# Two products in place of one fp32 product for three column sums, and a new place for evictions and conversions

## The chip, the core and the metric

One core of a Trainium2 chip runs the whole program. The metric is the device time in microseconds (us), the median of several executions. Engines: TensorE (PE, with its weight loads as PEld), ScalarE (ACT), VectorE (DVE), GpSimd (POOL), and SyncE (SP), which issues the transfers. ACT and DVE each work through their instructions in the order in which they stand.

## What is computed

Three stages follow each other: a chunked attention, a soft mixture of experts, and a feed-forward with a squared relu. Only the third is touched:

```
h = x @ w_in            # x: 3072 x 512, w_in: 512 x 2048
r = np.maximum(h, 0.0)
g = s * (r * r) + b
out = g @ w_out         # w_out: 2048 x 512
```

The kernel never forms x for this stage. x is c @ slot_out, with c the softmax over 32 slots of each token, so h = c @ (slot_out @ w_in). The small product slot_out @ w_in is called m. And since b is one number, g @ w_out = s * (r*r) @ w_out + b * (column sums of w_out).

## The kernel before

Tokens are cut into 8 blocks of 384, the 2048 hidden columns into 16 groups of 128. An item is one block with one group. The 128 items run in this order: blocks 0 and 1 in turn over groups 0 to 7, blocks 2 and 3 in turn over all 16, then blocks 4 to 7 one after the other, at last blocks 0 and 1 over groups 8 to 15. The loop over n near the end of the kernel is the order of everything: its step n emits, on each engine's own queue,

- PE: `emit_h(n)` (L825), one fp32r product h(n) of 384 columns into a bank of the PSUM tag `s`, which has two banks; then `emit_o(n-3)` (L877), six products of 512 columns (three token tiles with the high half `ghi` of the squares, three with the low half `glo`) against `w_hi`; then `emit_o2(n-4)` (L889), three more against `w_lo`. In the steps where a run over groups ends (n = 18 and 19, then 50, 51 and so on), or one step behind it (n = 20), `emit_o2` stands ahead of `emit_o`.
- ACT: relu (L831), the square (L835), the cast to `ghi` (L839).
- DVE: `glo` of item n-1, the square less its high half (L842).

So h(n) is written three steps ahead of its nine products. An h takes a bank of `s` that an earlier relu, or another reader, has released.

Beside this, w_out and the rest of w_in arrive as 64-bit numbers and are converted in the loop, one key every two steps until n = 47 (`cq`): `stage_a` is an ACT instruction (L579), `stage_d` parts 0 to 5 are DVE instructions (L589, L591, L593, L600 and, for w_out alone, L791 and L793), and `stage_w` is the ACT cast to `w_hi` (L798), which reads what L591 wrote. Keys n = 16 to 30 belong to w_in, n = 32 to 46 to w_out groups 8 to 15. `load_w` at the end of a step issues the next weight transfer once a step has read the last of an old one.

When a run over groups ends, the three accumulators of its block are evicted, two by DVE and one by ACT (L896, L894), and the next run's `emit_o` needs their banks.

The column sums that the title speaks of:

- m for 512 more hidden columns is made three times, at n = 4, 26 and 34 (`M_AT`). `emit_m` multiplies slot_out with w_in in four 32-row strips at once (L806, with a bf16 correction) into a bank of `s`; ACT copies it to `mps` (L808). One step later `emit_m2` adds the four strips by a product with a 128x128 pattern of ones, `stks_all`, in full fp32 (L812), into `s`; `m_split` then casts it to `mpack` on ACT (L817) and subtracts on DVE (L818). A product in full fp32 stands as two instructions in the trace, a product in fp32r as one.
- The column sums of w_out: DVE adds the 32 halves up in n = 48 to 63 (`wsum_add`, L848), and at n = 64 `colsum` multiplies by a 128x128 tile of ones in full fp32 (L852); DVE scales it to `bias` (L853).

In a step, before: h, o and o2 on PE, then `emit_m` or `emit_m2`, and only then that step's relu, square and so on. So ACT has the copy of `mps`, and the cast to `mpack`, ahead of the relu of its own step.

Of the kernel before, what the change touches and what calls it, by code (L numbers as in the profile page):

```python
# [8 lines left out]
F32 = mybir.dt.float32  # L9
F32R = mybir.dt.float32r  # L10
# [3 lines left out]
AF = mybir.ActivationFunctionType  # L14
ALU = mybir.AluOpType
# [20 lines left out]
def kernel(  # L36
# [11 lines left out]
    nc = tc.nc  # L48
# [3 lines left out]
    NT, DM = out.shape  # L52
# [9 lines left out]
    scale = 1.0 / 8.0  # L62
# [21 lines left out]
    stks_all = stk.rearrange("p a s -> p (a s)")  # L84
# [33 lines left out]
    with tc.manual_schedule():  # L118
# [45 lines left out]
        NRG, E_AT = 3, 5  # L164
        EARLY = [("wi", 2), ("wi", 3)]
        order = [("w1", i) for i in range(W1)] + [("wi", 0), ("wi", 1)] + [("w2", i) for i in range(W2)]
# [4 lines left out]
        order = order[0:-E_AT] + EARLY + order[-E_AT:]  # L171
# [9 lines left out]
        last_use = {}  # L181
# [7 lines left out]
        wnext = [0]  # L189
# [256 lines left out]
        def warm(n):  # L446
            wp = psum("lp", [128, 256])
            for _ in range(n):
                nc.tensor.matmul(out=wp, lhsT=warm_src[:, 0:128], rhs=warm_src, start=True, stop=True)
# [222 lines left out]
        def emit_sos(g, dh):  # L672
            nc.scalar.copy(out=sos_r[dh], in_=so_t[g, dh])
# [44 lines left out]
        for i in range(16):  # L718
            emit_w2(i)
            if i == 4:  # L720
                left.close()
                pk_p = ctx.enter_context(tc.tile_pool(name="pk", bufs=1, reuse_waits="tile"))
                cpack = pk_p.tile([128, NT], F32R, name="cpack")
                mpack = pk_p.tile([128, 128 * NF], F32R, name="mpack")
            if i in (3, 7, 11):
                emit_sos(i // 8, i // 4 % 2)
            if i in (4, 8, 12):
                emit_sot((i - 1) // 8, (i - 1) // 4 % 2)
            if i < 3:
                pack_prep(2 * i)  # L730
                pack_prep(2 * i + 1)
            if 5 <= i < 11:
                pack_c(i - 5)
            if i == 2:
                load_w(len(EARLY) + E_AT)
            if i == 10:
                load_w(2)
            if i == 14:
                load_w(1)
            if 11 <= i < 15:  # L740
                warm(4)
            if 7 <= i < 15:
                early(4 + (i - 7) // 2, (i - 7) % 2)

        LA = 3
        M_AT = (4, 26, 34)
# [4 lines left out]
        def tiles(name, n, w, dt=F32):  # L751
            return [g_p.tile([128, w], dt, name=f"{name}{i}") for i in range(n)]

        w_hi, w_lo = tiles("whi", NF, DM, F32R), tiles("wlo", NF, DM, F32R)
        os_g, mps = tiles("os", 3, DM), tiles("mps", 1, DM)[0]
        r_g, r2_g = (tiles(x, 2, UT) for x in ("r", "r2"))
        ghi_g, glo_g = tiles("ghi", LA + 2, UT, F32R), tiles("glo", LA + 2, UT, F32R)
        wsum, bias = tiles("wsum", 1, DM)[0], tiles("bias", 1, DM)[0]
        ones = tiles("ones", 1, 128)[0]
        nc.gpsimd.memset(ones, 1.0)  # L760
        HF = NF // 2

        runs = [[(0, 0, HF), (1, 0, HF)], [(2, 0, NF), (3, 0, NF)]]
# [18 lines left out]
        def stage_d(k, j):  # L782
            key = cq.get(k)
            if key:
                h, lf, a, w = cv[key]
                if j < 3:
                    cv_dve(key, j)
                elif j == 3:
                    cv_low(key, lf if key[0] == "o" else wi_dst([wis_l[:, 0:2], wis_l[:, 2:4]], key))
                elif key[0] == "o" and j == 4:  # L790
                    nc.vector.tensor_tensor(out=a, in0=a, in1=w_hi[key[1]].bitcast(F32), op=ALU.subtract)  # L791
                elif key[0] == "o":
                    nc.vector.tensor_tensor(out=w_lo[key[1]], in0=a, in1=lf, op=ALU.add)  # L793

        def stage_w(k):
            key = cq.get(k)
            if key and key[0] == "o":
                nc.scalar.copy(out=w_hi[key[1]], in_=cv[key][2])  # L798

        def emit_m(fb):  # L800
            wis = wis_b if fb % 2 else wis_a
            mp = psum("s", [128, 512])
            for lo in range(1 if fb == 1 else 2):
                for kc in range(KD):
                    lhsT, rhs = (soTb[:, kc, :], wis_l[:, kc, :]) if lo else (soT4[:, kc, 0, :], wis[kc // 2][:, kc % 2, :])
                    nc.tensor.matmul(out=mp[32 * kc:32 * kc + 32, :], lhsT=lhsT, rhs=rhs,  # L806
                                     start=(lo == 0), stop=(lo == 1 or fb == 1))
            nc.scalar.copy(out=mps, in_=mp)  # L808

        def emit_m2(fb):  # L810
            mr = psum("s", [128, 512])
            nc.tensor.matmul(out=mr, lhsT=stks_all, rhs=mps, start=True, stop=True)  # L812
            m_split(mr, 512 * fb, slice(0, 512))

        def m_split(mp, base, cols):
# [21 lines left out]
        def emit_ghi(n):  # L837
            if n < len(items):
                nc.scalar.copy(out=ghi_g[n % (LA + 2)], in_=r2_g[n % 2])  # L839
# [9 lines left out]

        def colsum():  # L850
            c = psum("s", [128, DM])
            nc.tensor.matmul(out=c, lhsT=ones, rhs=wsum, start=True, stop=True)  # L852
            nc.vector.tensor_scalar(out=bias, in0=c, scalar1=sbt[:, 1:2], scalar2=None, op0=ALU.mult)  # L853

        def store(b, t, os_):
# [24 lines left out]
        def emit_o2(n):  # L880
            r_, f = items[n]
            b, f0, f1 = r_
            ghi, glo = ghi_g[n % (LA + 2)], glo_g[n % (LA + 2)]
            for t in range(NTU):
                o = o_t[r_][t]
                if n == len(items) - 1:
                    for gt in (ghi, glo):
                        nc.tensor.matmul(out=o, lhsT=gt[:, 128 * t:128 * t + 128], rhs=w_hi[f], start=False, stop=False)
                nc.tensor.matmul(out=o, lhsT=ghi[:, 128 * t:128 * t + 128], rhs=w_lo[f], start=False, stop=(f == f1 - 1))  # L889
                if f == f1 - 1:  # L890
                    if b < 4 and f0 == 0:
                        to = part[b][t] if b < 2 else os_early(b - 2, t)
                        if t == 1:
                            nc.scalar.activation(out=to, in_=o, func=AF.Copy, scale=sbt[:, 0:1])  # L894
                        else:
                            nc.vector.tensor_scalar(out=to, in0=o, scalar1=sbt[:, 0:1], scalar2=None, op0=ALU.mult)  # L896
                    else:
                        os_ = os_g[t]
                        nc.vector.scalar_tensor_tensor(out=os_, in0=o, scalar=sbt[:, 0:1], in1=part[b][t] if f0 else bias,
                                                       op0=ALU.mult, op1=ALU.add)  # L900
                        store(b, t, os_)
# [12 lines left out]
        def stages(n, *js):  # L914
            for j in js:
                stage_d(n, j)


        cp = (nc.scalar.copy, nc.vector.tensor_copy)
        sot = psum("g", [128, 2, 4, 32])  # L920
# [3 lines left out]
        for k in range(2):  # L924
# [3 lines left out]
                  in_=sot[:, k:k + 1, :, 0:4].to_broadcast([128, 4, 4, 4]))  # L928
# [39 lines left out]
        for n in range(LA + 1, len(items) + LA + 1):  # L968
            if n > 7:
                emit_h(n)  # L970
            m = n - LA - 1
            ends = 0 <= m and items[m][1] == items[m][0][2] - 1
            late = m + 1 < len(items) and m + 1 == 2 * HF + 1
            if ends or late:
                emit_o2(m)
            if 1 < m + 1 < len(items):
                emit_o(m + 1)
            if m > 1 and not ends and not late:
                emit_o2(m)
            if LA + 1 < n <= 7:  # L980
                emit_h(n)
            if n == 6:
                nc.vector.tensor_copy(out=soTb, in_=soT4[:, :, 0, :])
            if n in M_AT:
                emit_m(M_AT.index(n) + 1)
            if n - 1 in M_AT:
                emit_m2(M_AT.index(n - 1) + 1)
            emit_relu(n)
            emit_sq(n)
            stage_a(n + 1)  # L990
            emit_ghi(n)
            if LA + 1 < n <= len(items):
                emit_g(n - 1)
            stage_d(n, 1)
            stage_w(n)
            stages(n, 2, 3)
            stages(n - 1, 4, 5)
            stage_d(n + 1, 0)
            if 48 <= n < 64:
                for i in (2 * n - 96, 2 * n - 95):  # L1000
                    wsum_add(i)
            if n == 64:
                colsum()
            if 65 <= n < 77:
                add_bias(n - 65)
            while wnext[0] < len(order) and last_use.get(order[wnext[0] - NRG], -1) <= n:
                load_w(1)


# [70 lines left out]
```

## Time and profile before

| | us |
|---|---|
| median of 3 executions | 480.83 |
| lowest and highest | 479.24, 481.24 |
| the profiled execution: its time | 479.52 |
| its span, first to last instruction | 477.7 |
| busy in the span: PE, ACT, DVE, POOL | 456.7, 308.7, 310.1, 84.4 |

The times are those of whole executions; the span is what the trace covers, here 1.8 us less than that execution's own time. Busy time on PE counts matmuls whose ends the profile models. A row of the timeline gives the start in us, the duration in us, the engine, the line, the tiles as out<-in, and in brackets how long the engine had stood idle and who ended it. `x2` or `x4` says that rows in a row were merged.

### The profile page before, as it was taken

What the parts mean: (1) busy time and instruction counts of PE and PEld (TensorE: products, weight loads), DVE (VectorE), ACT (ScalarE), POOL (GpSimd) and SP (SyncE); (2) the same over time, 40 slices, a digit from 0 to 9 for tenths busy, and PEclk for the clock granted to TensorE, in tenths of its full rate; (3) what the DMA queues carried; (4) which work ended last, traced back from release to release, by engine and by line L of the source; (5) the groups of instructions that cost most, each with busy time, mean ns of one, the idle gap of its engine ahead of it and who ended that gap; (6) DMA issues with size and microseconds to landing.
All of it is one profiled execution on the core that took longest, in us unless ns stands there. A gap on an engine that the chain in (4) does not pass through costs nothing.

```text
span 477.7 us, 10206 instructions
## 1 busy us (share of the span) xinstructions
PE 456.7 (96%) x3960; PEld 342.3 (72%) x3960; DVE 310.1 (65%) x685; ACT 308.7 (65%) x635; POOL 84.4 (18%) x154
## 2 busy tenths in 40 slices
PE   7899998999999999999898999999999999999996
PEld 5666666665555467868585888888888888888885
DVE  6778887885485889997484999975524224223232
ACT  4566666675144388888576897666666666666660
POOL 6666665650000000000000000007700000000000
PEclk9999999999999999999999999999999999999999
DMA  8999999999999934234222000003101001001011
GB/s 304 385 406 405 406 409 398 397 381 396 401 420 392 414 128 151 89 99 166 88 89 88 1 1 0 1 0 146 55 0 67 0 1 67 0 1 66 1 67 66
DMA packets 20576, 83.04 MB, mean 174 GB/s; under 512 B 2736, under 2 KB 2864, under 8 KB 14640
## 3 DMA queue, kind: packets, MB, share of 16 engines
q1 hardware_dynamic: 20528, 82.39, 44.6%
q8 instruction: 31, 0.51, 0.4%
q14 instruction: 17, 0.14, 0.1%
HBM read 76.09 MB, written 6.29 MB: 172 GB/s over the span
## 4 chain that ended last, share of the span: by engine, by line
PE 69%; DVE 13%; DMA 8%; ACT 4%; issue 3%; SPq 2%; POOL 1%; DVEq 0%; POOLq 0%; ACTq 0%
PE g L877 11%; PE lp L877 5%; PE pt L877 5%; PE x L877 5%; PE g L889 5%; PE xt L877 5%; PE s L825 4%; DMA seg<-in_w_dram 4%; PE s L630 3%; PE x L325 3%; DMA vals<-in_vm_dram 3%; PE lp L889 3%; PE pt L889 3%; PE xt L889 3%; PE x L889 3%
## 5 line engine op out<-in xcount | busy, mean ns | idle before, releaser
L842 DVE TENSOR_TENSOR glo<-r,ghi 128x384 fp32r<-128x384 f32 x128 | 76.3, 601 | 81.6 <-ACT ghi L839 81.4
L831 ACT ACTIVATE r<-s 128x384 f32<-128x384 f32 x128 | 62.8, 491 | 52.8 <-PE s L825 52.4
L835 ACT ACTIVATE r<-r 128x384 f32<-128x384 f32 x128 | 67.4, 527 | 6.2 <-DVE glo L842 2.0
L839 ACT CAST ghi<-r 128x384 fp32r<-128x384 f32 x128 | 65.7, 513 | 3.4
L825 PE MATMUL s<-cpack,mpack 128*128 128x384 f32 x128 | 44.2, 348 | 3.7 <-ACT r L831 2.1
L301 ACT ACTIVATE seg<-seg 128x384 f32<-128x384 f32 x32 | 28.8, 900 | 19.2 <-DVE seg L312 15.1
L889 PE MATMUL g<-wlo,ghi 128*128 128x512 f32 x128 | 40.2, 394 | 0.0
L877 PE MATMUL g<-whi,ghi 128*128 128x512 f32 x126 | 39.7, 394 | 0.2 <-DVE mpack L818 0.2
L877 PE MATMUL g<-whi,glo 128*128 128x512 f32 x126 | 39.3, 393 | 0.0
L864 POOL TENSOR_TENSOR keys<-keys,bias 128x512 f32<-128x512 f32 x6 | 8.4, 1426 | 168.7 <-DVE bias L853 168.7
L263 POOL TENSOR_SCALAR keys<-keys 64x416 f32<-64x416 f32 x63 | 33.7, 536 | 12.7 <-DMA keys<-in_kq_dram 7.5
L285 PE MATMUL s<-keys 128*32 128x128 f32 x768 | 30.3, 291 | 4.4 <-POOL keys L267 3.4
L825 PEld LDWEIGHTS s<-cpack,mpack 128*128 128x128 f32 x128 | 23.9, 188 | 13.0 <-ACT r L831 4.4
L325 PE MATMUL x<-vals,seg 128*32 128x128 f32 x744 | 28.0, 275 | 2.8 <-DMA vals<-in_vm_dram 2.0
L325 PEld LDWEIGHTS x<-vals,seg 128*32 128x32 f32 x744 | 20.3, 109 | 13.2 <-DVE seg L309 6.4
L889 PEld LDWEIGHTS g<-wlo,ghi 128*128 128x128 f32 x128 | 24.0, 188 | 5.3
L877 PEld LDWEIGHTS g<-whi,glo 128*128 128x128 f32 x126 | 23.7, 188 | 5.3
L285 PEld LDWEIGHTS s<-keys 128*32 128x32 f32 x768 | 19.5, 113 | 10.4 <-POOL keys L267 6.0
L319 ACT COPY seg<-pt 128x384 f32<-128x384 f32 x32 | 15.3, 478 | 17.9 <-PE pt L317 16.9
L877 PEld LDWEIGHTS g<-whi,ghi 128*128 128x128 f32 x126 | 23.7, 188 | 4.3 <-DVE mpack L818 0.7
L877 PE MATMUL lp<-whi,ghi 128*128 128x512 f32 x63 | 25.5, 404 | 0.9 <-DVE vals L896 0.9
L877 PE MATMUL pt<-whi,ghi 128*128 128x512 f32 x64 | 25.6, 400 | 0.0
(255 smaller groups left out, 991.1 us busy)
## 6 DMA issues: line engine op xcount, KB each, us to landing
seg<-in_w_dram SPq DMA_DIRECT2D x27, 1024.0 KB, 8.5
keys<-in_kq_dram SPq DMA_DIRECT2D x32, 396.0 KB, 7.4
vals<-in_vm_dram SPq DMA_DIRECT2D x64, 192.0 KB, 6.5
keys<-in_w_in_dram SPq DMA_DIRECT2D x5, 1024.0 KB, 5.1
keys<-in_w_out_dram SPq DMA_DIRECT2D x5, 1024.0 KB, 4.9
out_dram<-os SPq DMA_DIRECT2D x18, 256.0 KB, 2.1
vals<-in_w_in_dram SPq DMA_DIRECT2D x3, 1024.0 KB, 5.6
vals<-in_w_out_dram SPq DMA_DIRECT2D x3, 1024.0 KB, 4.9
```

Source lines behind the costliest of these rows:

```text
L263: (nc.vector if h and u == 0 else nc.gpsimd).tensor_scalar(out=stream(kz[rows, h], 0, CH), in0=k[rows, UT * h:UT * h + (NCU + 1) * CH].rea ...
L285: nc.tensor.matmul(out=o, lhsT=qt[:, 32 * c:32 * c + 32], rhs=kz[:, :, at:at + WIN], start=True, stop=not (first or last))
L301: nc.scalar.activation(out=p_r[u], in_=sm_r[u].rearrange("p t h (a r) -> p t r (h a)", a=2), func=AF.Exp, scale=scale)
L319: nc.scalar.copy(out=pts_r[u], in_=pt)
L325: nc.tensor.matmul(out=xp[32 * r:32 * r + 32, t], lhsT=pts_r[u][:, 32 * c:32 * c + 32], rhs=vbuf[u // 2 % 2][:, u % 2, :, 64 * c:64 * c + ...
L825: nc.tensor.matmul(out=hq, lhsT=mpack[:, 128 * f:128 * f + 128], rhs=cpack[:, b * UT:(b + 1) * UT], start=True, stop=True)
L831: nc.scalar.activation(out=r_g[n % 2], in_=h_t.pop(n), func=AF.Relu)
L835: nc.scalar.activation(out=r2_g[n % 2], in_=r_g[n % 2], func=AF.Square)
L839: nc.scalar.copy(out=ghi_g[n % (LA + 2)], in_=r2_g[n % 2])
L842: nc.vector.tensor_tensor(out=glo_g[n % (LA + 2)], in0=r2_g[n % 2], in1=ghi_g[n % (LA + 2)].bitcast(F32), op=ALU.subtract)
L877: nc.tensor.matmul(out=o_t[r_][t], lhsT=gt[:, 128 * t:128 * t + 128], rhs=w_hi[f], start=(f == r_[1] and gt is ghi), stop=False)
L889: nc.tensor.matmul(out=o, lhsT=ghi[:, 128 * t:128 * t + 128], rhs=w_lo[f], start=False, stop=(f == f1 - 1))
```

## The change

Four edits.

1. The strip sums at n = 26 and 34 and the column sums of w_out at n = 64 become two fp32r products (`sum_of`). `halves` makes the operand: ACT casts to fp32r (`mph`), DVE subtracts that from the source (`mpl`). The stationary patterns are held as fp32r too, `stkr` and `onesr`; ACT writes them earlier, in step i = 4 of the loop over w2 in the second stage. The sum at n = 4 keeps its fp32 product and only copies into `os_g[0]` instead of `mps`.
2. For n > 7, `emit_m` and `emit_m2` (now `sums`) are emitted behind that step's relu, square, `stage_a` and `ghi`, and ahead of `glo` and of the conversion.
3. The conversion of n = 18 (`convert`) and the weight load behind it move to step 19, behind the `emit_o2` that ends the second run and its evictions.
4. `bias` takes the memory of `wsum`; POOL no longer writes a tile of ones.

```diff
+                stkr = pk_p.tile([128, 128], F32R, name="stkr")
+                onesr = pk_p.tile([128, 128], F32R, name="onesr")
+                nc.scalar.copy(out=stkr, in_=stks_all)
+                nc.scalar.activation(out=onesr, in_=stks_all, func=AF.Copy, scale=0.0, bias=1.0)
...
-        os_g, mps = tiles("os", 3, DM), tiles("mps", 1, DM)[0]
+        os_g, (mph, mpl) = tiles("os", 3, DM), tiles("mp", 2, DM, F32R)
...
-        wsum, bias = tiles("wsum", 1, DM)[0], tiles("bias", 1, DM)[0]
-        ones = tiles("ones", 1, 128)[0]
-        nc.gpsimd.memset(ones, 1.0)
+        wsum = tiles("wsum", 1, DM)[0]
+        bias = wsum
...
-            nc.scalar.copy(out=mps, in_=mp)
+            if fb == 1:
+                nc.scalar.copy(out=os_g[0], in_=mp)
+            else:
+                halves(mp)
+
+        def halves(x):
+            nc.scalar.copy(out=mph, in_=x)
+            nc.vector.tensor_tensor(out=mpl, in0=x, in1=mph.bitcast(F32), op=ALU.subtract)
+
+        def sum_of(out, lhsT):
+            for x in (mph, mpl):
+                nc.tensor.matmul(out=out, lhsT=lhsT, rhs=x, start=(x is mph), stop=(x is mpl))
...
-            nc.tensor.matmul(out=mr, lhsT=stks_all, rhs=mps, start=True, stop=True)
+            if fb == 1:
+                nc.tensor.matmul(out=mr, lhsT=stks_all, rhs=os_g[0], start=True, stop=True)
+            else:
+                sum_of(mr, stkr)
...
-            nc.tensor.matmul(out=c, lhsT=ones, rhs=wsum, start=True, stop=True)
+            halves(wsum)
+            sum_of(c, onesr)
...
+        def convert(n):
+            stage_d(n, 1)
+            stage_w(n)
+            stages(n, 2, 3)
+            stages(n - 1, 4, 5)
+            stage_d(n + 1, 0)
...
+            if n == 2 * HF + 3:
+                convert(n - 1)
             if 1 < m + 1 < len(items):
                 emit_o(m + 1)
...
-            if n in M_AT:
-                emit_m(M_AT.index(n) + 1)
-            if n - 1 in M_AT:
-                emit_m2(M_AT.index(n - 1) + 1)
+            if n <= 7:
+                sums(n)
             emit_relu(n)
             emit_sq(n)
             stage_a(n + 1)
             emit_ghi(n)
+            if n > 7:
+                sums(n)
...
-            stage_d(n, 1)
...
+            if n != 2 * HF + 2:
+                convert(n)
...
-            while wnext[0] < len(order) and last_use.get(order[wnext[0] - NRG], -1) <= n:
+            while n != 2 * HF + 2 and wnext[0] < len(order) and last_use.get(order[wnext[0] - NRG], -1) <= n:
```

How the instructions stand on the engines, at the places the prediction speaks of. ACT at n = 34 and 35, before: the copy to `mps` is first, then the three instructions of item 34 (relu, square, ghi), the cast to `w_hi`, the cast to `mpack`, and relu of item 35.

```order
L808 COPY mps_2657<-s 128x512
L831 ACTIVATE r_2658<-s 128x384
L835 ACTIVATE r_2660<-r_2658 128x384
L839 CAST ghi_2666<-r_2660 128x384
L798 CAST whi_2631<-keys 128x512
L817 CAST mpack<-s 128x512
L831 ACTIVATE r_2659<-s 128x384
```

The same place now:

```order
L848 ACTIVATE r_2663<-s 128x384
L852 ACTIVATE r_2665<-r_2663 128x384
L856 CAST ghi_2671<-r_2665 128x384
L817 CAST mp_2661<-s 128x512
L801 CAST whi_2635<-keys 128x512
L848 ACTIVATE r_2664<-s 128x384
L852 ACTIVATE r_2666<-r_2664 128x384
L579 ACTIVATE seg_99<-keys 128x512
L856 CAST ghi_2667<-r_2666 128x384
L834 CAST mpack<-s 128x512
```

Item 34 now comes ahead of the evicting cast, and item 35 ahead of `mpack`; the cast to `w_hi` stays ahead of relu of item 35.

DVE at n = 33 and 34 now (before, the row L818 is not there and the rest stands in the same order): `glo` of item 33 and the conversion of key 34 (L591, L593, L600) come behind the subtraction that makes `mpl`.

```order
L589 TENSOR_SCALAR keys<-keys 128x512
L818 TENSOR_TENSOR mp_2662<-s,mp_2661 128x512
L859 TENSOR_TENSOR glo_2675<-r_2666,ghi_2670 128x384
L591 SCALAR_TENSOR_TENSOR keys<-vals_103,keys 128x512
L593 TENSOR_SCALAR keys<-keys 128x512
L600 SCALAR_TENSOR_TENSOR keys<-vals_103,keys 128x512
L835 TENSOR_TENSOR mpack<-s,mpack 64x512
```

So on DVE a wait for ACT's cast, and through it for `emit_m`, now stands ahead of L591, whose result ACT's cast to `w_hi` needs.

DVE at the end of the first two runs (n = 18 to 20), before: the evictions of the second run (`lp`, `g`) stand behind the conversion of key 18.

```order
L896 TENSOR_SCALAR part_2678<-xt,cstt 128x512
L842 TENSOR_TENSOR glo_2669<-r_2661,ghi_2664 128x384
L591 SCALAR_TENSOR_TENSOR seg_99<-keys 128x2x256
L593 TENSOR_SCALAR keys<-seg_99 128x512
L600 SCALAR_TENSOR_TENSOR seg_101<-keys 128x2x256
L896 TENSOR_SCALAR vals_104<-lp,cstt 128x512
L896 TENSOR_SCALAR vals_104<-g,cstt 128x512
L842 TENSOR_TENSOR glo_2670<-r_2660,ghi_2665 128x384
```

Now:

```order
L914 TENSOR_SCALAR part_2680<-xt,cstt 128x512
L859 TENSOR_TENSOR glo_2674<-r_2666,ghi_2669 128x384
L914 TENSOR_SCALAR vals_104<-lp,cstt 128x512
L914 TENSOR_SCALAR vals_104<-g,cstt 128x512
L591 SCALAR_TENSOR_TENSOR seg_99<-keys 128x2x256
L593 TENSOR_SCALAR keys<-seg_99 128x512
L600 SCALAR_TENSOR_TENSOR seg_101<-keys 128x2x256
L859 TENSOR_TENSOR glo_2675<-r_2665,ghi_2670 128x384
```

The two evictions have passed the three conversion instructions; the rows around the five are the same.

## Rows read from the trace of the kernel before

**Rows 1.** Busy us by engine (count), then PEclk, DMA share, GB/s, two stretches.

```profile
226.50:260.00 33.50, 30.00 (x140) 21.51 (x139) 19.70 (x36) 21.38 (x45) 0.00 (x0) 1.00 0.27 94
260.00:287.00 27.00, 27.00 (x121) 22.29 (x120) 26.38 (x51) 23.92 (x49) 0.00 (x0) 1.00 0.00 1
```

**Rows 2.** Timeline: start, us, engine, line, tiles [idle before]; h(26), its follower.

```profile
226.85 0.34 PE L825 MATMUL s<-cpack,mpack 128*128 128x384 f32 x1
227.02 0.40 PE L877 MATMUL lp<-whi,ghi 128*128 128x512 f32 x1
```

**Rows 3.** Timeline of steps 26 to 28: m, h(27), the strip sum, h(28).

```profile
230.08 0.40 PE L806 MATMUL s<-seg 128*32 128x512 bf16 x4
230.52 0.59 ACT L808 COPY mps<-s 128x512 f32<-128x512 f32 x1 [3.54 <-PE s L806]
231.16 0.45 PE L825 MATMUL s<-cpack,mpack 128*128 128x384 f32 x1 [0.68 <-ACT mps L808]
231.44 0.40 PE L877 MATMUL pt<-whi,ghi 128*128 128x512 f32 x1
...
233.50 1.02 PE L812 MATMUL s<-mps,stk 128*128 128x512 f32 x2
234.56 0.59 ACT L817 CAST mpack<-s 128x512 fp32r<-128x512 f32 x1 [1.96 <-PE s L812]
235.18 0.69 DVE L818 TENSOR_TENSOR mpack<-s,mpack 64x512 fp32r<-64x512 f32 x1 [3.97 <-ACT mpack L817]
235.59 0.44 PE L825 MATMUL s<-cpack,mpack 128*128 128x384 f32 x1 [1.07 <-ACT r L831]
```

**Rows 4.** Timeline of steps 34 to 39: h(34), a conversion, h(36), h(39), relus 37, 38.

```profile
249.24 0.34 PE L825 MATMUL s<-cpack,mpack 128*128 128x384 f32 x1
249.89 0.68 DVE L591 SCALAR_TENSOR_TENSOR keys<-vals,keys 128x512 int32<-128x512 int32 x1
254.90 0.62 ACT L798 CAST whi<-keys 128x512 fp32r<-128x512 f32 x1
258.01 0.44 PE L825 MATMUL s<-cpack,mpack 128*128 128x384 f32 x1 [1.07 <-ACT r L831]
262.18 0.48 ACT L831 ACTIVATE r<-s 128x384 f32<-128x384 f32 x1
264.10 0.48 ACT L831 ACTIVATE r<-s 128x384 f32<-128x384 f32 x1
264.87 0.34 PE L825 MATMUL s<-cpack,mpack 128*128 128x384 f32 x1
```

**Rows 5.** Timeline of steps 18 to 21: key 18, evictions, the next run, h(21).

```profile
211.28 0.69 DVE L591 SCALAR_TENSOR_TENSOR seg<-keys 128x512 int32<-128x512 int32 x1
212.62 0.40 PE L889 MATMUL xt<-wlo,ghi 128*128 128x512 f32 x1
213.07 0.75 DVE L896 TENSOR_SCALAR vals<-lp,cstt 128x512 f32<-128x512 f32 x1
213.73 0.74 DVE L896 TENSOR_SCALAR vals<-g,cstt 128x512 f32<-128x512 f32 x1
213.87 0.50 PE L877 MATMUL lp<-whi,ghi 128*128 128x512 f32 x1 [0.85 <-DVE vals L896]
214.38 0.55 DVE L842 TENSOR_TENSOR glo<-r,ghi 128x384 fp32r<-128x384 f32 x1
215.56 0.34 PE L825 MATMUL s<-cpack,mpack 128*128 128x384 f32 x1
```

**Rows 6.** Timeline of step 64: ghi(64), the column sums, the product behind h(65).

```profile
322.83 0.51 ACT L839 CAST ghi<-r 128x384 fp32r<-128x384 f32 x1
323.63 1.02 PE L852 MATMUL s<-wsum,ones 128*128 128x512 f32 x2
324.66 0.39 PE L877 MATMUL pt<-whi,ghi 128*128 128x512 f32 x1
```

**Rows 7.** Timeline of the second stage where the two patterns are now written.

```profile
146.85 0.33 ACT L684 COPY keys<-g 128x64 f32<-128x64 f32 x2 [0.83 <-PE g L679]
```

More of the change, by code (lines that the diff above doesn't have):

```diff
@@ L916, in stages, with sums @@
                 stage_d(n, j)
+        def sums(n):
+            if n in M_AT:
+                emit_m(M_AT.index(n) + 1)
+            if n - 1 in M_AT:
+                emit_m2(M_AT.index(n - 1) + 1)
+        def convert(n):
[4 more added lines that the diff above has]
+            stage_d(n + 1, 0)
         cp = (nc.scalar.copy, nc.vector.tensor_copy)
@@ L991 @@
             emit_ghi(n)
+            if n > 7:
+                sums(n)
             if LA + 1 < n <= len(items):
                 emit_g(n - 1)
-            stage_d(n, 1)
[L995 to L998, printed above, removed]
+            if n != 2 * HF + 2:
+                convert(n)
             if 48 <= n < 64:
```

## The prediction, made before the changed kernel ran

> **What bounds the kernel now.** I read the table of stretches first. From 260 to 287 us PE is busy all 27.00 us, and DVE 26.38; from 226.5 to 260, where two sums of m fall, PE is idle 3.50 of 33.50, at the full clock (1.00, that is 2.4 GHz) [rows 1]. So PE sets the time, and what a change takes off PE's queue, busy or idle, comes off the end, as long as ACT and DVE keep up. Then I read the timeline at the four places that the diff touches and looked at what PE waits for.
>
> The units first. From h(36) to h(39) are three steps in 6.86 us [rows 4], of which 0.11 is the late start of a stalled h: after a stall the next product follows h by 0.28 (231.16 to 231.44 [rows 3]), otherwise by 0.17 [rows 2]. So a step takes 2.25, and each of its nine 512-column products (2.25 - 0.17) / 9 = 0.23. On ACT and DVE an instruction that doesn't read its forerunner starts some 0.09 before that one's recorded end (0.75 long, next 0.66 later [rows 5]); one that waits for another engine starts 0.03 behind it, PE about 0.05 behind.
>
> **A: the end of the first two runs, n = 18 to 20.** PE finishes the products of `emit_o2(16)` at 212.62 + 0.23 = 212.85, but starts the next run at 213.87, because DVE evicts `lp` at 213.07 and `g` at 213.73, behind the three instructions of key 18 that began at 211.28 [rows 5]. Now the evictions take the place of those three: `lp` 211.28 to 212.03, `g` 211.94 to 212.68. Both are over before PE asks for them (212.85 and, two products later, 213.31). Then h(21) follows six products later, at 212.85 + 6 x 0.23 = 214.23, instead of 215.56: **1.33 gained**. DVE's five instructions are the same five, so `glo` at 214.38 stays; its user, the fourth product behind h(21), comes at 214.23 + 0.17 + 0.69 = 215.09, just behind its end at 214.93. Key 18 is finished 1.3 us later, and the weight load behind it moves on SP's queue by as much; nobody reads that buffer for several steps. Nothing below zero, then; the ends are 0 and 1.33.
>
> **B: the sum at n = 26.** The last part of `emit_m` starts at 230.08, and PE could go on about 0.25 later, say at 230.35. Before, h(27) waits for the copy of `mps` and its next product comes at 231.44 [rows 3]. Now the bank that h(27) takes is released by relu(26), which runs during step 26, while ACT had 3.54 idle. So h(27) starts at 230.35, the next product at 230.52: 0.92 won. Nine products later, at 232.60, PE comes to the strip sum. By then `mph` is cast (230.52 plus 0.59, by L817's row) and `mpl` subtracted (231.14 to 231.83, by L818's row, 0.69 for 64 partitions; L591's 0.68 on all 128 says that partitions don't matter) [rows 3, 4]: 0.7 to spare. The two products take 0.46; the fp32 one with h behind it took 324.66 - 323.63 = 1.03, so 0.86 by itself [rows 6], and 0.40 is saved. Then h(28) waited 1.07 for relu(27), which stood behind `mpack` [rows 3]; now relu(27) runs ahead of `mpack`, at about 231. So h(28) starts at 233.06 and its follower at 233.23, where it was 235.59 + 0.28 = 235.87: **2.64 gained** in all.
>
> **C: the sum at n = 34.** The same, with one difference: w_out's key 34 is converted here. T = 249.24 is h(34), against 226.85 [rows 2, 4], so m's cast starts at 249.24 + 3.67 = 252.91 and `mpl` runs from 253.53 to 254.22. Behind it on DVE are `glo`(33) from 254.13 (0.55) and L591 from 254.59 (0.68) to 255.27. Before, L591 ran at 249.89, long before `w_hi`'s cast at 254.90 [rows 4]. Now this cast waits until 255.30, takes 0.62, and relu(35) behind it runs from 255.83 to 256.31. h(36) waits for that, where PE could have had it at 255.45: h(36) at 256.36, follower 256.64, against 258.29 before: 1.65. Next, `mpack`: it stands where relu(36) stood, one relu, square, `stage_a` and `ghi` behind relu(35), 1.92 by relu(37) to relu(38) [rows 4], so at 257.75, and relu(36) ends at 258.25 + 0.48 = 258.73. h(37) takes the bank of h(36) (the banks go out in the order in which the code releases them), and wants it at 256.64 + 9 x 0.23 = 258.71: about on time. DVE's subtraction for `mpack` starts at 257.75 + 0.59 + 0.03 = 258.37, where before it started at 257.60 (0.41 ahead of h(36), as 235.18 is ahead of h(28) [rows 3]). So the DVE and ACT work behind it is 0.8 later while PE is 1.65 earlier. How much slack is there? relu(37) ended at 262.66 and h(39), which needs its bank, came at 264.87: 2.16 [rows 4]. 2.16 - 0.8 = 1.35, less than 1.65. So the gain here is capped at **1.35**. It doesn't shrink further: two steps of DVE work, seen as 26.38 in 27.00, still fit. Ends: 0.9 (the chain 0.45 later) and 2.64 (no chain, as in B); I take 1.35, which the rows of this very place give.
>
> **D: the column sums at n = 64.** Before, nothing is waited for: PE runs from `emit_o2` into the product at 323.63 [rows 6]. Now the cast of `wsum` stands behind `ghi`(64), which ends at 323.34: cast 323.25 to 323.87 (0.62, by the `w_hi` cast of the same size [rows 4]), subtraction 323.90 to 324.59, second product 324.64, h(65) at 324.98, its follower at 325.15 against 324.66: **0.49 lost**. The shorter product saves 0.40 and two waits cost 0.9. Ends: 0.3 and 0.7 lost.
>
> **E, at nothing.** ACT writes `stkr` and `onesr` in a place where it stood idle 0.83 for PE [rows 7]; each is smaller than a `ghi` cast of 0.51 [rows 6]. If that cover failed, up to 1.0 would be lost, though the stage ahead of the loop would have to be bound by ACT. POOL's missing tile of ones, the shared memory of `bias` and the other target of the first sum cost and save nothing: nobody waited for them.
>
> The sum: 1.33 + 2.64 + 1.35 - 0.49 = 4.83. Behind n = 65 PE has no other sum, and every later eviction moves along. The profiled execution's 479.52 becomes 474.7; it lay 1.31 below the median of the three, and against that median, 480.83, I predict **476.0**. Half a per cent, 2.4 us, is about what a measurement of this kernel can tell from no change.
>
> **The rivals.** *The halves come too late.* In place of `mps` PE waits for `mpl`, a chain through two engines. For it: two more links, and DVE has other work queued. Against it: 0.7 to spare in B. Each us beyond that costs one us in B and in C; with 1.0 in each, 2.8 are left: 478.0.
>
> *The evictions change nothing.* If PE's bank at 213.87 is held by something else than the two evictions (ACT's third of the second run, say), A gives 0: 3.5 left, 477.3. The brackets name DVE [rows 5].
>
> *The cast to `w_hi` holds nobody.* If C goes like B, 6.1 are gained: 474.7. The order of the rows speaks against it.
>
> *DVE and ACT are the bound.* DVE's 26.38 of 27.00 [rows 1] speaks for it: then what PE wins by n = 34 it loses again by n = 47, waiting for relu and `glo`, and about 1 us is left of it all: 480. Against it: the slack of 2.16 that h(39) still has.
>
> *Slower: the clock.* The trace shows 1.00 through every stall there is now, the longest 1.07 on PE [rows 1, 3]. The changed kernel has a new one at D, up to 0.7, and shorter ones elsewhere. Should the granted clock fall there to 1.2 GHz, nine products would take 9 x 0.23 = 2.1 us more per step, and three steps, some 13 us at the low level, would cost 6.3: 482.3. From 4.83 / 2.1 = 2.3 steps on the kernel is slower than before. The Trainium skill (TensorE: Matmul & The Clock Gate, section "Why this matters for your kernels") warns that idle gaps between bursts of matmuls drop the clock to half; the trace's stalls did not, and the new ones are no longer.
>
> **How the numbers follow.** My forecast gets 0.58, the late halves 0.15, the idle evictions 0.10, the free `w_hi` cast 0.08, DVE and ACT as the bound 0.06, the clock 0.03. The first four lie between 474.3 and 478.3 with the ends above (C at 0.9 and 2.64, D at 0.3 and 0.7) and the spread of the runs, and hold about 8 in 10; that is the range. All four are faster by more than 2.4 us but for the tail of the late halves: 0.88 faster, 0.09 within half a per cent (DVE and ACT as the bound, and that tail), 0.03 slower.
>
> **What would show it.** A: no idle time on PE ahead of the run that starts in `lp`, and h(21) 1.3 earlier behind h(20). B: h(27) and h(28) without idle time, h(26) to h(28) in 6.2 instead of 8.74. C: idle time of some 0.9 ahead of h(36), put down to a relu, and `w_hi`'s cast waiting for L591; a little ahead of h(37) to h(39). D: PE idle 0.3 and 0.4 ahead of the two products. I am wrong if PE waits for `mpl` at n = 27 or 35, or if idle time on PE between n = 37 and 47 adds up to over 1 us.

## The result, and the profile after

| | before | after |
|---|---|---|
| median, us (6 executions each) | 480.39 | 475.42 |
| lowest and highest, us | 479.24, 481.32 | 474.58, 476.47 |
| the profiled execution: its time, its span, us | 479.52, 477.7 | 475.71, 473.9 |
| h(17) starts, us | 204.72 | 205.60 |
| from there to the end of the span, us | 272.98 | 268.30 |

The ratio of the times is 0.990, with a 95% interval of 0.988 to 0.992: faster by 4.97 us, and by the interval 3.8 to 5.9. The loop from h(17) on is 4.68 shorter; the profiled execution shows only 3.81 of that because its loop began 0.88 later (experiment f0 below takes this up).

The stretches that answer [rows 1], from just ahead of h(26) to just ahead of h(37) and 27 us on; columns as there:

```profile
226.04:255.46 29.42, 28.80 (x140) 21.61 (x139) 18.33 (x35) 20.91 (x44) 0.00 (x0) 1.00 0.23 77
255.46:282.46 27.00, 27.00 (x121) 21.84 (x119) 26.36 (x49) 22.04 (x46) 0.00 (x0) 1.00 0.08 35
```

The same eleven steps take 29.42 us, where they took 33.50, and PE stands idle 0.62 of it, not 3.50; the clock stays at 1.00 in both. The next stretch has PE busy throughout and DVE at 26.36, as before.

The view of waits, for PE, from 200 to 330 us (engine, line, who ended the wait: us in total, times, longest). Before:

```profile
PE s L825 <- ACT r L831: 2.1, 2, 1.1
PE s L825 <- ACT mps L808: 1.4, 2, 0.7
PE lp L877 <- DVE vals L896: 0.9, 1, 0.9
```

After:

```profile
PE s L842 <- ACT r L848: 0.6, 1, 0.6
PE s L822 <- DVE mp L818: 0.2, 1, 0.2
```

All five waits before are gone; two short ones are new, one for relu(35) and one for `mpl` at n = 64. Now the four places. The end of the first two runs, which answers [rows 5]:

```profile
212.14 0.75 DVE L914 TENSOR_SCALAR vals<-lp,cstt 128x512 f32<-128x512 f32 x1
212.80 0.74 DVE L914 TENSOR_SCALAR vals<-g,cstt 128x512 f32<-128x512 f32 x1
213.46 0.69 DVE L591 SCALAR_TENSOR_TENSOR seg<-keys 128x512 int32<-128x512 int32 x1
213.72 0.39 PE L895 MATMUL lp<-whi,ghi 128*128 128x512 f32 x1
215.08 0.34 PE L842 MATMUL s<-cpack,mpack 128*128 128x384 f32 x1
```

The evictions end at 212.89 and 213.54, L591 comes behind them, and the run that starts in `lp` has no idle time in brackets.

The sum at n = 26 to 28, which answers [rows 3]:

```profile
229.62 0.40 PE L809 MATMUL s<-seg 128*32 128x512 bf16 x4
229.95 0.44 PE L842 MATMUL s<-cpack,mpack 128*128 128x384 f32 x1
230.06 0.59 ACT L817 CAST mp<-s 128x512 fp32r<-128x512 f32 x1 [1.70 <-PE s L809]
230.23 0.40 PE L895 MATMUL pt<-whi,ghi 128*128 128x512 f32 x1
230.68 0.69 DVE L818 TENSOR_TENSOR mp<-s,mp 128x512 fp32r<-128x512 f32 x1 [4.11 <-ACT mp L817]
232.28 0.64 PE L822 MATMUL s<-mp,stkr 128*128 128x512 f32 x2
232.75 0.34 PE L842 MATMUL s<-cpack,mpack 128*128 128x384 f32 x1
```

Neither h(27) at 229.95 nor h(28) at 232.75 waits, and `mpl` ends at 231.37, 0.91 ahead of the products.

The sum at n = 34, which answers [rows 4]: L591 of key 34, the cast to `w_hi`, relu(35), h(36), `mpack`, relu(36), `mpack`'s subtraction, then the cast of key 36, relu(37), h(39):

```profile
251.65 0.68 DVE L591 SCALAR_TENSOR_TENSOR keys<-vals,keys 128x512 int32<-128x512 int32 x1
252.37 0.62 ACT L801 CAST whi<-keys 128x512 fp32r<-128x512 f32 x1 [1.82 <-DVE keys L591]
252.90 0.48 ACT L848 ACTIVATE r<-s 128x384 f32<-128x384 f32 x1
253.43 0.44 PE L842 MATMUL s<-cpack,mpack 128*128 128x384 f32 x1 [0.62 <-ACT r L848]
254.79 0.58 ACT L834 CAST mpack<-s 128x512 fp32r<-128x512 f32 x1
255.27 0.49 ACT L848 ACTIVATE r<-s 128x384 f32<-128x384 f32 x1
255.40 0.69 DVE L835 TENSOR_TENSOR mpack<-s,mpack 64x512 fp32r<-64x512 f32 x1 [1.88 <-ACT mpack L834]
259.44 0.62 ACT L801 CAST whi<-seg 128x512 fp32r<-128x512 f32 x1 [1.60 <-DVE seg L591]
259.96 0.48 ACT L848 ACTIVATE r<-s 128x384 f32<-128x384 f32 x1
260.50 0.44 PE L842 MATMUL s<-cpack,mpack 128*128 128x384 f32 x1
```

ACT stands 1.82 for L591, and relu(35) behind its cast keeps h(36) waiting. Behind the late subtraction of `mpack`, L591 of key 36 is late too: its cast waits 1.60, and relu(37) behind it is over at 260.44, 0.06 ahead of h(39), which takes its bank. The column sums at n = 64, which answer [rows 6]:

```profile
318.93 0.61 ACT L817 CAST mp<-wsum 128x512 fp32r<-128x512 f32 x1
319.57 0.69 DVE L818 TENSOR_TENSOR mp<-wsum,mp 128x512 fp32r<-128x512 f32 x1 [2.22 <-ACT mp L817]
319.59 0.49 PE L822 MATMUL s<-mp,onesr 128*128 128x512 f32 x1
320.32 0.50 PE L822 MATMUL s<-mp,onesr 128*128 128x512 f32 x1 [0.23 <-DVE mp L818]
```

The first product comes 0.51 behind the start of the product ahead of it (319.08), where 0.23 is usual, and the second 0.73 behind the first: 0.28 and 0.50 late. The brackets show less, since they count from the modelled end of the product ahead.

### The profile page after: what moved, and what is told of

It is laid out like the page before. It is cut to its first block, busy times and chain, and to the rows that moved or that the text cites. A ratio compares the mean times of both kernels' runs of the same rounds, so it can differ in the third digit from the quotient of the medians.

```text
span 473.9 us, 10204 instructions
## 1 busy us (share of the span) xinstructions
PE 455.1 (96%) x3960; PEld 342.1 (72%) x3960; DVE 311.3 (66%) x688; ACT 308.0 (65%) x638; POOL 83.9 (18%) x153
## 4 chain that ended last, share of the span: by engine, by line
PE 73%; DMA 12%; DVE 6%; ACT 3%; SPq 2%; POOL 2%; issue 1%; DVEq 0%; POOLq 0%; ACTq 0%
PE g L895 12%; PE lp L895 6%; PE pt L895 6%; PE g L907 6%; PE x L895 6%; DMA vals<-in_vm_dram 6%; PE xt L895 6%; PE s L842 5%; DMA seg<-in_w_dram 3%; PE pt L907 3%; PE s L630 3%; PE lp L907 3%; PE xt L907 3%; PE x L907 3%; DMA keys<-in_kq_dram 3%; PE x L325 2%
## 5 line engine op out<-in xcount | busy, mean ns | idle before, releaser
L882 POOL TENSOR_TENSOR keys<-keys,wsum 128x512 f32<-128x512 f32 x6 | 8.4, 1422 | 193.8 <-DVE wsum L871 193.8
L907 PE MATMUL pt<-wlo,ghi 128*128 128x512 f32 x64 | 25.4, 396 | 0.2 <-DVE wlo L796 0.2
```

## The experiments

The difference of two medians is known to about 1 us either way here (e1's interval is 1.8 us wide, f3's 3.5), but one timeline gives a stretch of the loop to some 0.04: that is the most by which A to D differ between kernels that the edits leave alike there. So each kernel is read twice: by its time, and by five lengths out of its own timeline. A is h(20) to h(21); B is h(26) to the product that follows h(28); C is h(34) to the product that follows h(39); D is h(64) to the product that follows h(66); "loop" is h(17) to the end of the span, known to some 0.05, as the page gives the span to 0.1. All in us:

| kernel | A | B | C | D | loop | h(17) starts |
|---|---|---|---|---|---|---|
| before | 3.58 | 9.03 | 15.81 | 5.53 | 272.98 | 204.72 |
| after | 2.23 | 6.54 | 14.49 | 6.04 | 268.30 | 205.60 |
| e1, evictions alone | 2.26 | 9.02 | 15.77 | 5.52 | 271.66 | 205.64 |
| e2, order alone | 3.58 | 6.93 | 13.70 | 5.53 | 268.76 | 205.34 |
| e3, fp32r alone | 3.56 | 9.03 | 15.79 | 6.02 | 273.44 | 204.86 |
| e4, after, key 34 first | 2.24 | 6.54 | 13.29 | 6.04 | 267.10 | 207.90 |
| f0, after once more | 2.24 | 6.54 | 14.50 | 6.04 | 268.30 | 207.00 |
| f1, order and evictions | 2.23 | 6.93 | 13.70 | 5.53 | 267.41 | 205.79 |
| f2, after, late column sums | 2.24 | 6.54 | 14.50 | 5.17 | 267.41 | 205.59 |
| f3, after, both mends | 2.23 | 6.54 | 13.30 | 5.17 | 266.29 | 206.91 |

The first four ran on one chip, with a before of 480.56 (median of 23), the last four on another with 479.50 (median of 11).

**e1: the evictions alone.** On the kernel before:

```diff
+            if n == 2 * HF + 3:
+                convert(n - 1)
             if 1 < m + 1 < len(items):
                 emit_o(m + 1)
...
+            if n != 2 * HF + 2:
+                convert(n)
```

> The kernel before with the third edit alone: key 18's conversion and the weight load behind it stand behind the evictions of the second run. Theory: the 1.35 us that the changed kernel gained between h(20) and h(21) belong to this edit, so h(20) to h(21) takes 2.23 instead of 3.58 and the whole time falls by 1.35, to 479.0 from 480.4. Rival, that the gain needs the other edits or is given back behind n = 21: no change, 480.4.

Measured: 478.94, ratio 0.997 (0.995 to 0.999). A falls by 1.32 and the loop by 1.32; B, C and D are as before (to 0.04). In PE's waits the row for `lp` is gone and the two rows for h remain as they were. So edit 3 carries A by itself, and nothing of it is given back.

**e2: the order alone.** On the kernel before, with `mps` and all products in full fp32:

```diff
+            if n <= 7:
+                sums(n)
             emit_relu(n)
             emit_sq(n)
             stage_a(n + 1)
             emit_ghi(n)
+            if n > 7:
+                sums(n)
```

> The kernel before with the second edit alone: the sums of m at n = 26 and 34 stand behind relu, square and ghi; all three products stay full fp32, and no high and low part is made. Theory: the place of the sums carries the gain at both of them. At n = 26 the changed kernel won 2.48 us from h(26) to the follower of h(28); the fp32 product costs 0.40 more, so 2.1 here. At n = 34 no subtraction stands ahead of L591, so w_hi's cast doesn't wait and it goes as at n = 26: 2.1. Together 4.2, 476.2 us. Rival, that the late mpack caps the gain at n = 34 here too (1.36 less 0.40): 3.0, 477.4. Rival, that the two fp32r products carry the gain: under 1, above 479.5.

Measured: 475.94, ratio 0.991 (0.990 to 0.993). B falls by 2.10, C by 2.11, the loop by 4.22; the rivals would have shown 3.0 or under 1. From n = 22 to 64 PE's view of waits has no row left. Why C does as well as B stands in ACT's and PE's timeline at n = 34 to 36:

```profile
251.42 0.59 ACT L808 COPY mps<-s 128x512 f32<-128x512 f32 x1 [1.69 <-PE s L806]
251.90 0.62 ACT L798 CAST whi<-keys 128x512 fp32r<-128x512 f32 x1
252.42 0.49 ACT L831 ACTIVATE r<-s 128x384 f32<-128x384 f32 x1
253.65 1.02 PE L812 MATMUL s<-mps,stk 128*128 128x512 f32 x2
254.10 0.74 PE L825 MATMUL s<-cpack,mpack 128*128 128x384 f32 x1
```

The cast to `w_hi` follows the copy without a wait, relu(35) is over at 252.91, and h(36) at 254.10 follows the sum at once. The order alone wins more at C (2.11) than the whole change does (1.32).

**e3: the fp32r products alone,** in the old place; the changed kernel without edits 2 and 3:

```diff
-            if n <= 7:
-                sums(n)
+            sums(n)
             emit_relu(n)
...
-            if n > 7:
-                sums(n)
```

> The kernel before with the first and the fourth edit alone: two fp32r products with a high and a low part at n = 26, 34 and 64, in the old place ahead of relu. Theory: the products by themselves win nothing. Each strip sum is 0.40 shorter, but h(27) and h(35) now wait for the subtraction (0.69 behind the cast) or for the relu behind the cast (0.4 later) where they waited for the cast alone: 0 to 0.3 lost at each; at n = 64 0.48 is lost as in the changed kernel. Together 0.5 to 1.1 slower than before: 480.9 to 481.5 us. Rival, that the shorter products count in full: 0.8 won, 0.48 lost, 480.1.

Measured: 480.27, ratio 1.001 (0.999 to 1.002). By the time it can't be told from before; the loop is 0.46 longer, just below the 0.5 to 1.1 expected, and all of it lies in D (0.49). B and C are unchanged to 0.02. The timeline at n = 26 to 28:

```profile
230.63 0.58 ACT L817 CAST mp<-s 128x512 fp32r<-128x512 f32 x1 [3.55 <-PE s L809]
231.11 0.50 ACT L848 ACTIVATE r<-s 128x384 f32<-128x384 f32 x1
231.66 0.44 PE L842 MATMUL s<-cpack,mpack 128*128 128x384 f32 x1 [1.07 <-ACT r L848]
234.00 0.63 PE L822 MATMUL s<-mp,stkr 128*128 128x512 f32 x2
235.71 0.44 PE L842 MATMUL s<-cpack,mpack 128*128 128x384 f32 x1 [1.07 <-ACT r L848]
```

h(27) now waits 1.07 for the relu behind the cast, where it waited 0.68 for the copy [rows 3]: 0.39 lost, which the shorter sum wins back.

**e4: key 34 first.** On the changed kernel, L591 of key 34 ahead of `mpl`'s subtraction:

```diff
             if n > 7:
+                if n == M_AT[2]:
+                    stage_d(n, 1)
                 sums(n)
...
-            stage_d(n, 1)
+            if n != M_AT[2]:
+                stage_d(n, 1)
```

> The changed kernel with L591 of key 34 on DVE ahead of the subtraction that makes mpl at n = 34, not behind it and glo(33). Theory: w_hi's cast waited 1.82 us for L591, and held relu(35) and so h(36) (idle 0.62); that made the gain at n = 34 only 1.36 where n = 26 gave 2.48. Without it h(34) to the follower of h(36) goes as h(26) to that of h(28), 6.54 instead of 7.42, and 1.1 us is won over the changed kernel: 474.3. Rival, that mpack, which still stands ahead of relu(36), or DVE's load caps it at n = 34 to 39: 475.4, as the changed kernel.

Measured: 475.58, ratio 0.991 (0.989 to 0.993); the median is no better than the changed kernel's, against 474.3 expected. But C is 1.20 shorter and the loop 1.20; what hides it is h(17), which began at 207.90 in the profiled execution (and at 206.7 in the median of the six, worked out as under f0, against 205.3 in the changed kernel). ACT, DVE and PE at n = 34 to 36:

```profile
252.71 0.62 ACT L801 CAST whi<-keys 128x512 fp32r<-128x512 f32 x1
252.85 0.69 DVE L818 TENSOR_TENSOR mp<-s,mp 128x512 fp32r<-128x512 f32 x1 [3.37 <-ACT mp L817]
254.45 0.64 PE L822 MATMUL s<-mp,stkr 128*128 128x512 f32 x2
254.92 0.34 PE L842 MATMUL s<-cpack,mpack 128*128 128x384 f32 x1
```

The cast waits for nobody, `mpl` still ends 0.91 ahead of the products, and h(36) comes without a wait. `mpack` stands ahead of relu(36) here too, and DVE has the same work; neither costs anything. So the wait of one cast for one DVE instruction was all that kept C under B.

**f0: the changed kernel once more.**

> The changed kernel once more, beside the three that follow. By theory all of its gain lies in the loop, from h(17) to the end of the span: 4.7 us less than the 272.98 of before. When h(17) starts (204.72 before, 205.60 after, 204.86 to 207.90 in the four experiments so far, with and without the two patterns) is set by the last waits of the second stage for its weights, and differs from run to run; so the median comes out 4.2 to 5.2 below before. Rival, that the two new patterns delay the loop: h(17) lies later here than in the kernels without them, and the median gain falls short of the loop's.

Measured: 475.81, ratio 0.991 (0.989 to 0.994), 3.69 below this chip's before of 479.50: less than the 4.2 to 5.2 expected, which is what the rival would show. Its loop is 268.30, equal to that of the first profile to 0.01 (the traces hold the two spans as 475.308 and 473.898), though h(17) began 1.40 later. If the loop is that constant, each execution's span less the loop of its kernel tells when its h(17) began: 204.2 to 209.9, median 205.75, in 42 executions of kernels with the two patterns, and 204.1 to 208.2, median 205.44, in 57 without. A difference of 0.3 is less than one execution differs from the next. But the two chips disagree: on the first, e3 and e4 with the patterns have a median of 205.5, and before, e1 and e2 without them 205.6; on the second, f0, f2 and f3 have 206.1, and before and f1 205.0. So the times alone don't settle whether the patterns cost anything. The timelines say more. Waits of PE late in the second stage, before, after and in e4, one row from each:

```profile
161.73 1.07 PE L668 MATMUL xt<-seg,seg 128*32 128x256 f32 x16 [0.28 <-DMA seg<-in_w_dram]
```

```profile
162.57 1.07 PE L668 MATMUL xt<-seg,seg 128*32 128x256 f32 x16 [0.83 <-DMA seg<-in_w_dram]
```

```profile
159.88 1.07 PE L668 MATMUL xt<-seg,seg 128*32 128x256 f32 x16 [1.18 <-DMA seg<-in_w_dram]
```

They are waits for the weights of the second stage, which differ from run to run: in all 0.6 before, 1.2 after and 3.0 in e4. They are not the whole of it: in f0 PE is 1.05 of the 1.40 behind already at 142.90, its row of 141.85 in the first profile, ahead of these waits. One thing there differs between profiles: the granted clock of the first 20 us is 0.83 in e2, e4, f0, f1 and f3, and 1.00 in the other five. And ACT in the changed kernel, where the patterns are written, which answers [rows 7]:

```profile
146.85 0.30 ACT L727 CAST stkr<-stk 128x128 fp32r<-128x128 f32 x1 [0.54 <-PE xt L668]
147.05 0.31 ACT L728 ACTIVATE onesr<-stk 128x128 fp32r<-128x128 f32 x1
147.26 0.31 ACT L684 COPY keys<-g 128x64 f32<-128x64 f32 x2
148.73 0.58 ACT L653 CAST cpack<-lp 128x512 fp32r<-128x512 f32 x1 [1.16 <-PE lp L651]
```

The two take 0.4 together, and ACT stands idle 1.16 for PE soon after. PE was 0.29 later than before at its row of 138.98 (138.69 before), ahead of the patterns, and is 0.29 later at 161.13 (160.84 before), behind them: between the two nothing is lost. The other profiles agree: from PE's row that waits for ACT's L632 (141.55 before) to its first L449 (157.49 before), with the patterns' place between them, it takes 15.93 to 15.95 in all ten. So PE loses nothing to the two patterns in this stretch. Why h(17) lies later with them on the second chip stays open; no run has the patterns alone.

**f1: order and evictions, no halves.** The edits of e1 and e2 together on the kernel before.

> The second and third edit together on the kernel before, all products in full fp32 as before: the changed kernel without its high and low parts. Theory: the fp32r products lose more than they win. The order alone gave 2.10 at n = 26 and 2.12 at n = 34, the evictions 1.32, and n = 64 costs nothing: 5.5 over before, 0.8 more than the changed kernel: 474.9 where before has 480.4. Rival, that the parts add up to less when put together, or that the fp32r products pay: 475.6 or above.

Measured: 474.49, ratio 0.988 (0.986 to 0.991). The loop is 5.57 shorter than before and 0.89 shorter than the changed kernel's. The parts add up (1.32 + 4.22 = 5.54), and the fp32r products as the change has them cost: 0.39 won in B, 0.79 lost in C, 0.51 in D.

**f2: late column sums.** On the changed kernel:

```diff
         def colsum():
             c = psum("s", [128, DM])
-            halves(wsum)
             sum_of(c, onesr)
...
             if n == 64:
+                halves(wsum)
+            if n == 65:
                 colsum()
```

> The changed kernel with the two products of the column sums one step later, at n = 65; the cast and the subtraction stay at n = 64. Theory: the 0.48 lost at n = 64 were two waits of 0.9 for the cast and the subtraction against 0.40 saved; a step later both halves are long done, h(64) to the follower of h(66) goes without a wait, and the loop is 0.9 shorter than in the changed kernel: 474.6. Rival, that the cast ahead of relu(65), or a bank of s held until the scaling to bias, brings the wait back: 475.4, as the changed kernel.

Measured: 475.38, ratio 0.991 (0.989 to 0.994). The median, expected at 474.6, again can't be told from the changed kernel's; the loop is 0.89 shorter, all of it in D:

```profile
318.91 0.62 ACT L817 CAST mp<-wsum 128x512 fp32r<-128x512 f32 x1
319.56 0.69 DVE L818 TENSOR_TENSOR mp<-wsum,mp 128x512 fp32r<-128x512 f32 x1 [2.22 <-ACT mp L817]
321.56 0.64 PE L822 MATMUL s<-mp,onesr 128*128 128x512 f32 x2
322.03 0.34 PE L842 MATMUL s<-cpack,mpack 128*128 128x384 f32 x1
```

The halves are made at the same time as in the changed kernel and are over at 320.25, 1.3 ahead of the products, which now run without a wait. Against before D is 0.36 shorter: that is the fp32r product's own saving.

**f3: both mends,** the edits of e4 and f2 on the changed kernel.

> The changed kernel with both mends: L591 of key 34 ahead of the subtraction, and the column sums' products at n = 65. Theory: evictions 1.35, n = 26 2.48, n = 34 2.51, n = 64 0.40: 6.7 in the loop, 2.0 more than the changed kernel: 473.7 where before has 480.4. Rival, that DVE or ACT becomes the bound once PE is no longer held: the waits of PE between n = 36 and 64 then give back what the mends win, 475.4.

Measured: 474.42, ratio 0.989 (0.985 to 0.992), where 473.7 was expected from a before of 480.4 (here it was 479.50). The loop is the shortest of all, 2.01 less than the changed kernel's and 6.69 less than before. The stretches from just ahead of h(26) to just ahead of h(37), and 27 us on:

```profile
227.36:255.86 28.50, 28.50 (x140) 21.66 (x139) 18.95 (x35) 21.13 (x44) 0.00 (x0) 1.00 0.23 77
255.86:282.86 27.00, 27.00 (x121) 22.30 (x120) 26.36 (x51) 22.32 (x46) 0.00 (x0) 1.00 0.09 37
```

PE is busy all of both, and its view of waits has no row from 200 to 325 us; DVE at 26.36 of 27.00 still holds nobody. f3's loop is 1.12 shorter than f1's, so with the two waits moved the fp32r products do pay. By the median f1 and f3 can't be told apart, nor f3 from the changed kernel with certainty; both are faster than before.

## Why the prediction was right, point by point

Forecast 4.83 off, measured 4.97 by the medians and 4.68 in the loop. The mechanism held at all four places. That the medians come within 0.14 of the forecast is luck in part: their interval spans 2 us, and h(17) alone moves by more from one execution to the next. What bears the forecast out are the lengths A to D.

- **A**, 1.33 forecast, 1.35 in the timeline, 1.32 with edit 3 alone. The rival that something else held PE's bank falls: the row for `lp` went with the move.
- **B**, 2.64 forecast, 2.49 measured. h(27) and h(28) wait for nobody, as said, and `mpl` has 0.91 to spare where 0.7 was reckoned, so the rival of late halves falls. By e2 the order alone gives 2.10 of it, and the shorter product the other 0.39. What was mis-sized is a term of 0.44: from the last part of `emit_m` to the product behind h(27) I reckoned 0.27 and 0.17, the rows give 0.61 (229.62 to 230.23). The h behind those parts is followed as late as a stalled one (0.28), though no wait is put down for it.
- **C**, 1.35 forecast, 1.32 measured, and each link as worked out. From h(34), `w_hi`'s cast was to end at 6.68, relu(35) to start at 6.59, h(36) at 7.12, `mpack` at 8.51, its subtraction at 9.13; the rows give 6.70, 6.61, 7.14, 8.50, 9.11. The idle time ahead of h(36) is 0.62 and not 0.9, because PE came to it some 0.15 later, which is what B lacks, and because the profile counts from the modelled end of the product ahead (252.18 + 0.63). From h(34) to the product behind h(36) the gain is 1.63 (1.65 forecast), and 0.31 of it goes again up to h(39), which is held by relu(37) and followed after 0.28, as said. e4 adds what the trace of before could not: this one wait is the whole cause, and `mpack` ahead of relu(36) only passes it on. The rival in which the cast holds nobody falls in the changed kernel, and is what e2 and e4 show when L591 runs ahead.
- **D**, 0.49 lost by forecast, 0.51 measured. The two halves of that, 0.40 saved and 0.9 of waits, are 0.36 and 0.87 by f2. The sign named for it, idle time of 0.3 and 0.4, is in the starts of the two products (0.28 and 0.50 late) and not in the brackets, which show 0.23 ahead of the second alone.
- **E**, nothing by forecast. The ten profiles show nothing lost on PE where the patterns are written; by the times of whole executions it is open, from nothing on one chip to 1.1 on the other.
- *DVE and ACT as the bound*: but for h(37) and h(39), some 0.1 late in the changed kernel, a `glo` product behind h(37), 0.05 late, and the halves at n = 64, PE waits for neither from n = 37 to 65, at 26.36 of 27.00. *The clock*: 1.00 from 195 to 473 us, the waits at n = 36 and 64 among it; so no run here shows what a fall to 1.2 GHz in the loop would cost.

What the forecast left unasked is whether the high and low parts are worth having. It priced their losses at C and D and their gain at B, but one by one; the sum of those prices is already a loss, and f1's loop shows it as 0.89.

The Trainium skill (FP8 and Floating Point Precision, section "TensorE Precision Notes") gives a true fp32 product four passes. By that, two fp32r products of 0.23 save two passes, an estimate of 0.46; the runs show somewhat less, 0.39 in B and 0.36 in D.

## What to carry to other kernels

Ahead of speeding up an instruction on the busiest engine, ask which engine's queue holds its operand and its bank: here the place of the sums in ACT's queue was worth 4.2 us at two sums, and the faster product 0.4 a time. A product split in high and low parts puts a second engine between producer and consumer, so place the parts a step ahead of the product, and look at what else waits behind them on that second engine. Where the end of an earlier stage scatters by a us, compare lengths inside the timelines, not medians.

## What the runs showed of the hardware that was not expected

- The fixed part repeats far better than the time: two profiles of one kernel have the same 268.30 from h(17) to the end, while h(17) moves by up to 5 us between executions of one kernel (204.6 to 209.9 in f3, worked out as in f0). The profiles show two things that differ there, the waits for the second stage's weights (0.6 to 3.0 us in all) and the granted clock of the first 20 us (1.00 or 0.83; in f0, where PE was busy 0.8 of the 3 us ahead, it stands at 0.50, the level of 1.2 GHz, from 9 to 14 us; in the first profile of this kernel, busy 1.6 of the same 3 us, at 1.00). How much each moves h(17) in the executions without a profile isn't shown.
- Behind products in 32-row strips the next full product comes 0.33 after the start of the last strip group and its follower 0.28 after that, with no releaser in the trace (229.62, 229.95, 230.23); behind other products the follower comes after 0.17. The trace names no other engine as the one that PE waits for, so the cause stays open.
